# Attention and two feed-forward layers on one core: the first two blocks issued in another written order, their copies on ScalarE, products of zeros before the first scores

## The chip, the cores and the metric

The kernel runs on 1 core of one Trainium2 chip. The metric is the device time of one execution in microseconds (us), as the median over runs. A core has TensorE (PE; its weight loads are shown as PEld), VectorE (DVE), ScalarE (ACT), GpSimd (POOL) and SyncE (SP), whose queue issues all the DMAs here. Each engine works through its own queue in order and waits on semaphores.

## What is computed

Three functions in a row, on 4 x 576 = 2304 tokens, in float32 (the weights arrive as float64):

```python
x = attention(q, k, v)             # 8 heads of 64; heads 0-3: a local window of 32 keys,
                                   # heads 4-7: keys of the same residue mod 32; causal
h = x @ w_in;  x = (h - tanh(h)) @ w_out             # 512 -> 2048 -> 512
xn = x / sqrt(mean(x*x) + 1e-6) * rms_g
out = (silu(xn @ w_gate) * (xn @ w_val)) @ w_out2    # 512 -> 1536 -> 512
```

## The kernel before

The tokens are cut into nine blocks of 256, and the blocks into groups (0,1), (2,3), (4), (5,6), (7,8). For each group the attention of its blocks makes `xs`, and the first feed-forward layer then runs over 16 slices f of 128 columns of `w_in`: a unit (g, f, a, e) is `pe_h` (12 products into `ps_h`), `act_tanh`, `dve_g`, `g_hi` (ScalarE), `g_lo` (VectorE), and `pe_x` (12 products with a slice of `w_out` into `ps_x`). To keep float32 precision every operand stands as a high part (a copy in fp32r) and a low part (the rest), and a product is three: high by high, high by low, low by high.

A weight is converted while group 0 is worked on, one 128 x 512 slice at a time. `Weight.bits`: a scaling of the raw bits (`ca`, on GpSimd for the first five, on ScalarE later), then three operations on VectorE (lines 169 to 173) that put the 32 bits together (`ct`). `Weight.split`: the high part by ScalarE (line 181), the low part by VectorE (line 182). In group 0, 32 slices go this way.

Attention of a block has a local half L and a strided half D, and each half has two items 0 and 1. The stages of a half are `st_s` (scores on TensorE, preceded for the first two blocks by two products with the identity that write the mask), `st_m` (maxima, VectorE, lines 283 to 291), `st_e` (exponentials, ScalarE, line 297), `st_n` (normalisation, VectorE, lines 305 to 307), `st_p` (transposes, TensorE, line 316), `st_c` (copy out of the accumulators, line 320), `st_v` (products with v, TensorE) and `st_o` (lines 324 and 325: high part by ScalarE, low part by VectorE, into `xs`).

For the first two blocks the order is written out by hand: the string `START` is a list of words, and `first` issues them one after the other, under a manual schedule that keeps that order on each engine. `m0L1` is `st_m` of block 0, half L, item 1. Of the other words `<` lists the loads, B is the `bits` of the next weight, H its `split`, h the `pe_h` of the next unit, T its tanh and all that follows up to `g_lo`, X its `pe_x`. The last letters of p, s, v name the accumulator bank, those of c the engine. All that comes after `START` is placed by a scheduler, which also puts later work into gaps. The last two lines of the string:

```python
m1D0 e1D0 n1L0 p1L0h c1L0v T H m1D1 e1D1 n1L1 p1L1h c1L1v B h H X
n1D0 p1D0m c1D0v T n1D1 p1D1m c1D1v v1Lh o1L0 o1L1 v1Dh o1D0 o1D1 B h H T B
```

Of the kernel before, what the change touches and what calls it, by code (L numbers as in the profile page):

```python
# [32 lines left out]
def attn_moe_moe_kernel(  # L33
# [112 lines left out]
    class Weight:  # L146
# [9 lines left out]

        def bits(self, on_act):
            w = self.raw.rearrange("p c f -> p (c f)").bitcast(U32).rearrange("p (n t) -> p n t", t=2)
            lo, hi = w[:, :, 0], w[:, :, 1]
            a = cvt.tile([128, 512], F32, tag="ca", name="ca")  # L160
            if on_act:
                nc.scalar.mul(out=a, in_=hi.bitcast(F32), mul=2.0 ** -111)  # L162
            else:
                nc.gpsimd.tensor_scalar(
                    out=a, in0=hi.bitcast(F32), scalar1=2.0 ** -111, scalar2=1.0, op0=ALU.mult, op1=ALU.mult
                )
            a = a.bitcast(U32)
# [5 lines left out]
            nc.vector.scalar_tensor_tensor(  # L173
                out=t, in0=lo, scalar=29, in1=t, op0=ALU.logical_shift_right, op1=ALU.bitwise_or
            )
            self.b = t.bitcast(F32)

        def split(self, pool, tag, lo_eng):
            self.t = pool.tile([128, 2, 4, 128], F32R, tag=tag, name="w")
            t = self.t.rearrange("p s c f -> p s (c f)")  # L180
            nc.scalar.copy(out=t[:, 0], in_=self.b)  # L181
            lo_eng.tensor_tensor(out=t[:, 1], in0=self.b, in1=t[:, 0].bitcast(F32), op=ALU.subtract)  # L182

# [54 lines left out]
    class Heads:  # L238
# [586 lines left out]
    wks = [Work(groups[1])]  # L825
    xq, tq, pg = [], [], None
    banks = {"h": bank_h, "m": bank_m, "x": bank_x}
    eng = {"a": nc.scalar.copy, "v": nc.vector.tensor_copy}

    def first(word):  # L830

        op, rest = word[0], word[1:]
        if op == "<":
            for c in rest:
                loads[c]()
        elif op in "BH":
            if op == "B":
                st1.ws[st1.i].bits(False)
                st1.i += 1
            else:  # L840
                k = next(k for k, w in enumerate(st1.ws) if not hasattr(w, "t"))
                pool, tag, e = st1.place(k)
                st1.ws[k].split(pool, tag, e)
        elif op == "h":
            tq.append(units.pop(0))
            pe_h(*tq[-1])
        elif op == "T":
            u = tq.pop(0)
            for fn in (act_tanh, dve_g, g_hi, g_lo):
                fn(*u)  # L850
            xq.append(u)
        elif op == "X":
            pe_x(*xq.pop(0))
# [204 lines left out]
```

## Time and profile before

| | before |
|---|---|
| median of 3 runs | 972.84 us (972.03 to 973.92) |
| the profiled execution | 970.39 us, span of its instructions 968.6 us |
| busy, share of the span: PE, DVE, ACT, POOL | 95%, 60%, 35%, 17% |
| the chain that ended last: PE, DVE, DMA, POOL | 83%, 9%, 4%, 2% |
| instructions in the span | 13634 |

The span runs from the first to the last instruction of the profiled execution; 1.8 us of its time lie around the span. Busy TensorE counts each product with the whole time that it is in flight, and products overlap, so a stage in which TensorE is always busy need not be one in which it works at its peak. The granted clock of TensorE (PEclk) is 1.0 for 2.4 GHz and 0.5 for 1.2 GHz; there is no record of it before 22.6 us of this execution, and the views show 1.0 there.

### The profile page before, as it was taken

To read this page: it belongs to the slowest core of one execution; us is meant where nothing else is said; L and a number is where in the kernel's file an instruction comes from. 1 tells how busy PE (TensorE), PEld (TensorE's weight loads), DVE (VectorE), ACT (ScalarE), POOL (GpSimd) and SP (SyncE) were. 2 spreads that over 40 slices of the span, in tenths; PEclk is the share of its full clock that TensorE was granted. 3 is DMA by queue.
4 is the path that set the end of the run, shared out by engine and by line. 5 is a ranking of instruction groups with operands and counts; after the bars stand their busy time and mean duration, and the time that the engine had idled before them with its cause. 6 is when DMAs were issued, how large, how long until landed. Compare 5 with 4: busy or idle time off the path is not lost.

```text
span 968.6 us, 13634 instructions
## 1 busy us (share of the span) xinstructions
PE 920.4 (95%) x5242; PEld 762.5 (79%) x5242; DVE 579.8 (60%) x1270; ACT 343.0 (35%) x787; POOL 160.0 (17%) x216
## 2 busy tenths in 40 slices
PE   4589998799989999999999999999999999999998
PEld 2478776588879978888888888888888888888897
DVE  4569899998576898728999865245123512231212
ACT  3346664332245332336656423113111311121111
POOL 0000023678232767300000000000000000000000
PEclk9679999999999999999999999999999999999999
DMA  9536342331132210017536211101010000000000
GB/s 280 142 131 234 114 141 87 106 109 39 33 97 82 77 46 17 1 61 243 184 121 221 64 64 44 44 0 44 1 44 1 22 1 23 22 1 1 33 12 23
DMA packets 33731, 72.87 MB, mean 75 GB/s; under 512 B 6977, under 2 KB 15553, under 8 KB 33665
## 3 DMA queue, kind: packets, MB, share of 16 engines
q1 hardware_dynamic: 33664, 71.99, 22.9%
q8 instruction: 41, 0.67, 0.3%
q14 instruction: 26, 0.20, 0.1%
HBM read 62.54 MB, written 9.44 MB: 74 GB/s over the span
## 4 chain that ended last, share of the span: by engine, by line
PE 83%; DVE 9%; DMA 4%; POOL 2%; issue 1%; ACT 1%; SPq 0%; ACTq 0%; DVEq 0%
PE ps_x L142 32%; PE ps_h L142 32%; PE ps_m L142 16%; DVE so L523 2%; DMA raw<-in_w_in_dram 2%; POOL pr L483 2%; PE ps_v L142 1%; PE ps_p L316 1%; DVE g L674 1%; DMA raw<-in_w_out_dram 1%; PE ps_s L142 1%; DVE tg L663 1%; DVE w L182 1%; DVE sc L488 1%; DVE ct L173 1%
## 5 line engine op out<-in xcount | busy, mean ns | idle before, releaser
L142 PE MATMUL ps_x<-g,w 128*128 128x512 f32 (+1 forms) x984 | 218.3, 371 | 7.7 <-DVE w L182 4.4
L142 PE MATMUL ps_h<-xs,w 128*128 128x512 f32 (+1 forms) x984 | 222.1, 375 | 2.1 <-DVE w L182 1.1
L142 PEld LDWEIGHTS ps_x<-g,w 128*128 128x128 f32 x984 | 170.5, 191 | 40.4 <-DVE w L182 5.5
L142 PEld LDWEIGHTS ps_h<-xs,w 128*128 128x128 f32 x984 | 174.2, 196 | 34.5 <-ACT w L181 1.8
L773 DVE SCALAR_TENSOR_TENSOR s<-ps_m,s 128x512 f32<-128x512 f32 (+1 forms) x60 | 38.3, 638 | 222.4 <-PE ps_m L142 222.1
L142 PE MATMUL ps_h<-xn,w 128*128 128x512 f32 (+1 forms) x720 | 159.1, 369 | 0.0
L142 PE MATMUL ps_m<-xn,w 128*128 128x512 f32 (+1 forms) x720 | 158.4, 368 | 0.0
L142 PE MATMUL ps_x<-w,p 128*128 128x512 f32 x648 | 157.8, 391 | 0.0
L142 PEld LDWEIGHTS ps_h<-xn,w 128*128 128x128 f32 x720 | 126.8, 188 | 24.5
L142 PEld LDWEIGHTS ps_m<-xn,w 128*128 128x128 f32 x720 | 126.0, 188 | 23.1
L142 PEld LDWEIGHTS ps_x<-w,p 128*128 128x128 f32 x648 | 120.7, 188 | 25.6
L483 POOL TENSOR_TENSOR pr<-sk,sq 128x256 f32<-128x256 f32 (+1 forms) x101 | 84.2, 867 | 128.6 <-DMA sk<-in_k_str_dram 88.9
L772 ACT ACTIVATE s<-ps_h 128x512 f32<-128x512 f32 (+1 forms) x60 | 33.3, 556 | 163.6 <-PE ps_h L142 163.3
L516 POOL TENSOR_TENSOR pr<-sv,se 128x288 f32<-128x288 f32 (+12 forms) x104 | 71.2, 707 | 68.6 <-DVE so L523 20.3
L775 ACT CAST p<-s 128x512 fp32r<-128x512 f32 (+1 forms) x60 | 34.6, 577 | 122.5 <-DVE s L773 122.5
L669 ACT CAST g<-tg 128x512 fp32r<-128x512 f32 (+1 forms) x82 | 46.6, 568 | 87.2 <-DVE tg L663 86.9
L663 DVE SCALAR_TENSOR_TENSOR tg<-ps_h,tg 128x512 f32<-128x512 f32 (+1 forms) x82 | 50.7, 618 | 35.9 <-ACT tg L658 35.9
L658 ACT ACTIVATE tg<-ps_h 128x512 f32<-128x512 f32 (+1 forms) x82 | 44.5, 543 | 78.0 <-PE ps_h L142 77.7
L523 DVE TENSOR_REDUCE so<-pr 128x16 f32<-128x240 f32 (+11 forms) x104 | 64.8, 651 | 6.6 <-POOL pr L516 6.2
L674 DVE TENSOR_TENSOR g<-tg,g 128x512 fp32r<-128x512 f32 (+1 forms) x82 | 58.2, 709 | 12.3 <-ACT g L669 11.9
L776 DVE TENSOR_TENSOR p<-s,p 128x512 fp32r<-128x512 f32 (+1 forms) x60 | 38.3, 638 | 25.9 <-ACT p L775 25.6
L162 ACT ACTIVATE ca<-raw 128x512 f32<-128x512 f32 x63 | 42.4, 674 | 31.6 <-DVE ct L170 14.9
(77 smaller groups left out, 682.7 us busy)
## 6 DMA issues: line engine op xcount, KB each, us to landing
raw<-in_w_out_dram SPq DMA_DIRECT2D x28, 512.0 KB, 5.3
raw<-in_w_in_dram SPq DMA_DIRECT2D x16, 512.0 KB, 7.5
raw<-in_w_gate_dram SPq DMA_DIRECT2D x12, 512.0 KB, 3.6
raw<-in_w_val_dram SPq DMA_DIRECT2D x12, 512.0 KB, 3.5
x2d<-xe SPq DMA_DIRECT2D x36, 128.0 KB, 2.0
x<-x2d SPq DMA_DIRECT2D x16, 256.0 KB, 4.0
out_dram<-o SPq DMA_DIRECT2D x16, 256.0 KB, 2.0
sk<-in_k_str_dram SPq DMA_DIRECT2D x4, 576.0 KB, 3.8
```

What stands on the lines that cost most here:

```text
L142: nc.tensor.matmul(out_, lhsT, rhs, start=start, stop=stop, skip_group_check=True)
L162: nc.scalar.mul(out=a, in_=hi.bitcast(F32), mul=2.0 ** -111)
L483: nc.gpsimd.tensor_tensor(out=pr, in0=self.k[:, a:e, :], in1=self.q[:, c - c0:c - c0 + 1, :].to_broadcast([128, e - a, D]), op=ALU.mult,)
L516: nc.gpsimd.tensor_tensor(out=pr, in0=self.v[:, 0:c + 1, a:e], in1=self.e[:, c - c0, 0:c + 1].unsqueeze(2).to_broadcast([128, c + 1, e - a ...
L523: pend.append(lambda: nc.vector.tensor_reduce(out=o[:, c - g0, a:e], in_=pr.rearrange("l c d -> l d c"), axis=AX.X, op=ALU.add))
L658: nc.scalar.activation(out=t, in_=h_of[g, f, a], func=ACTF.Tanh, scale=WS)
L663: nc.vector.scalar_tensor_tensor(out=t, in0=h_of.pop((g, f, a)), scalar=WS, in1=t, op0=ALU.mult, op1=ALU.subtract)
L669: nc.scalar.copy(out=t[:, 0], in_=t_of[g, f, a])
L674: nc.vector.tensor_tensor(out=t[:, 1], in0=t_of.pop((g, f, a)), in1=t[:, 0].bitcast(F32), op=ALU.subtract)
L773: nc.vector.scalar_tensor_tensor(out=s, in0=r[1], scalar=WS, in1=s, op0=ALU.mult, op1=ALU.mult)
L775: nc.scalar.copy(out=t[:, 0], in_=s)
L776: nc.vector.tensor_tensor(out=t[:, 1], in0=s, in1=t[:, 0].bitcast(F32), op=ALU.subtract)
```

## The change

`START` is replaced by another list. The same words' work is in it, five scalings and five mergings of weights, four splits, three `pe_h`, three tanh and one `pe_x`, the eight copies, in another order and cut finer. B is now A (scaling, GpSimd) and B (the three VectorE operations); H is P (high part, ScalarE) and Q (low part, VectorE); T is T, G, I, J (tanh, `dve_g`, `g_hi`, `g_lo`); o is y (high part) and z (low part). Numbers after the letters name the weight or the unit. All eight copies c go to ScalarE; before, VectorE did them. The loads are in another order: the first raw weight comes after the v's of block 0 and not before them. A new word W9 clears a tile and multiplies it with itself nine times on TensorE (bf16, 128 x 512), ahead of all other products.

```diff
 START = """
-<tabwcdwAwBCDwwww2ww
-s0Lx s0Dx m0L0 e0L0 m0L1 e0L1 m0D0 e0D0 m0D1 e0D1 B
-n0L0 p0L0h c0L0v n0L1 p0L1h c0L1v H s1Lx n0D0 p0D0m c0D0v m1L0 e1L0
-v0Lh o0L0 o0L1 n0D1 p0D1m c0D1v m1L1 e1L1 v0Dh o0D0 o0D1 s1Dm h B
...
+<tabcdwABwCDwww2ww
+W9
+s0Lx m0L0 s0Dx m0L1 m0D0 e0L0 m0D1 e0L1 n0L0 p0L0h0 A0 e0D0 n0L1 B0 p0L1h1 c0L0a s1Lx c0L1a e0D1 n0D0 v0Lh0
+P0 n0D1 p0D0m0 y0L0 A1 p0D1m1 y0L1 z0L0 c0D0a z0L1 s1Dx c0D1a Q0 v0Dh1 m1L0 m1L1 y0D0 y0D1 z0D0 A2 e1L0 z0D1
+m1D0 h0h0 e1L1 n1L0 m1D1 p1L0m0 T0 G0 c1L0a n1L1 I0 e1D0 J0 p1L1m1 B1 c1L1a e1D1 n1D0 P1 n1D1 p1D0m0 Q1
+c1D0a p1D1m1 B2 v1Lm0 A3 c1D1a v1Dm1 y1L0 y1L1 z1L0 P2 h1h1 z1L1 y1D0 Q2 y1D1 z1D0 A4 X0 T1 z1D1 G1 h2h0 B3
+I1 T2 J1 P3 G2 Q3 I2 J2 B4
 """
...
+        elif op == "W":
+            z = att.tile([128, 512], F32, tag="sm", name="zero").bitcast(BF16)[:, :512]
+            nc.vector.memset(z, 0.0)
+            ps = bank_of("m0")("ps_w")
+            for _ in range(int(rest)):
+                mm(ps, z[:, :128], z, True, True)
...
+        elif op in "ABPQ":
+            w = st1.ws[int(rest)]
+            pool, tag, e = st1.place(int(rest))
+            if op == "A":
+                w.scale(nc.gpsimd)
...
             elif op == "c":
-                fn(int(rest[0]), eng[rest[1]])
+                fn(int(rest[0]), nc.scalar.copy)
```

`scale`, `merge`, `high`, `low`, `st_y` and `st_z` are the two halves of `bits`, `split` and `st_o`, with the same operations. Line numbers after line 21 are 3 to 34 higher in the changed kernel.

The order on VectorE around the first normalisations, before (names: `nm` maxima, `ct` and `ca` a weight's bits, `ss` and `sm` sums and exponentials, `ps_p` transposed, `pT` its copy):

```order
L283 TENSOR_REDUCE nm<-ps_s 128x2 x2
L291 TENSOR_SCALAR nm<-nm 128x4
L169 TENSOR_SCALAR ct<-ca 128x512
L170 SCALAR_TENSOR_TENSOR ct<-ca,ct 128x512
L173 SCALAR_TENSOR_TENSOR ct<-raw,ct 128x512
L305 TENSOR_SCALAR ss<-ss 128x4
L306 RECIPROCAL ss<-ss 128x4
L307 TENSOR_TENSOR sm<-sm,ss 128x384
L320 COPY pT<-ps_p 96x512
L305 TENSOR_SCALAR ss<-ss 128x4
L306 RECIPROCAL ss<-ss 128x4
L307 TENSOR_TENSOR sm<-sm,ss 128x384
```

and in the changed kernel:

```order
L298 TENSOR_REDUCE nm<-ps_s 128x2 x2
L306 TENSOR_SCALAR nm<-nm 128x4
L320 TENSOR_SCALAR ss<-ss 128x4
L321 RECIPROCAL ss<-ss 128x4
L322 TENSOR_TENSOR sm<-sm,ss 128x384
L320 TENSOR_SCALAR ss<-ss 128x4
L321 RECIPROCAL ss<-ss 128x4
L322 TENSOR_TENSOR sm<-sm,ss 128x384
L174 TENSOR_SCALAR ct<-ca 128x512
L175 SCALAR_TENSOR_TENSOR ct<-ca,ct 128x512
L178 SCALAR_TENSOR_TENSOR ct<-raw,ct 128x512
L320 TENSOR_SCALAR ss<-ss 128x4
```

The first weight has moved behind the two normalisations of half L, and the copy between them is gone from VectorE.

The order on TensorE from the last product with the mask of block 1's half L on, before (`lq` queries and keys, `v` and `dv` values of the halves L and D, `tab` the mask):

```order
L142 MATMUL ps_s<-tab 128x384
L142 MATMUL ps_s<-lq 64x96 x16
L316 MATMUL ps_p<-tab,sm 64x128 x4
L142 MATMUL ps_v<-pT,v 64x64 x16
L316 MATMUL ps_p<-tab,sm 64x128 x4
L142 MATMUL ps_v<-pT,dv 32x64 x32
```

and in the changed kernel:

```order
L145 MATMUL ps_s<-tab 128x384
L145 MATMUL ps_s<-lq 64x96 x16
L145 MATMUL ps_v<-pT,v 64x64 x16
L331 MATMUL ps_p<-tab,sm 64x128 x8
L145 LDWEIGHTS tab
L145 MATMUL ps_s<-tab 128x256
```

The products with `v` now come ahead of all eight transposes of half D, and where the products with `dv` stood the mask of block 1's half D begins, with the scores that follow it.

VectorE later in group 0, behind the written list, where the scheduler sets the order, before (`w` a weight's low part, `tg` and `g` of a unit):

```order
L169 TENSOR_SCALAR ct<-ca 128x512
L170 SCALAR_TENSOR_TENSOR ct<-ca,ct 128x512
L663 SCALAR_TENSOR_TENSOR tg<-ps_h,tg 128x512
L182 TENSOR_TENSOR w<-ct,w 128x512
L173 SCALAR_TENSOR_TENSOR ct<-raw,ct 128x512
L169 TENSOR_SCALAR ct<-ca 128x512
L674 TENSOR_TENSOR g<-tg,g 128x512
```

and in the changed kernel:

```order
L178 SCALAR_TENSOR_TENSOR ct<-raw,ct 128x512 x2
L696 TENSOR_TENSOR g<-tg,g 128x512
L189 TENSOR_TENSOR w<-ct,w 128x512 x2
L174 TENSOR_SCALAR ct<-ca 128x512 x2
L175 SCALAR_TENSOR_TENSOR ct<-ca,ct 128x512 x2
L685 SCALAR_TENSOR_TENSOR tg<-ps_h,tg 128x512
L178 SCALAR_TENSOR_TENSOR ct<-raw,ct 128x512
```

The weights, which took turns with a distance of half a conversion, now go through the same steps two by two.

## Rows read from the trace of the kernel before

**Rows 1.** The page's first part: busy time, share and instructions of each engine.
```profile
PE 920.4 (95%) x5242; PEld 762.5 (79%) x5242; DVE 579.8 (60%) x1270; ACT 343.0 (35%) x787; POOL 160.0 (17%) x216
```

**Rows 2.** Stages: busy us (instructions) of PE, PEld, DVE, ACT, POOL; PEclk, DMA, GB/s.
```profile
0.00:66.60 66.60, 38.54 (x448) 29.97 (x449) 36.47 (x110) 24.03 (x101) 4.57 (x11) 0.77 0.58 173
66.60:181.40 114.80, 104.96 (x702) 80.73 (x701) 107.43 (x250) 65.89 (x152) 22.43 (x24) 0.98 0.41 140
181.40:400.00 218.60, 212.57 (x1457) 181.79 (x1456) 176.73 (x469) 81.28 (x234) 133.03 (x181) 0.99 0.22 66
400.00:968.60 568.60, 564.37 (x2641) 470.07 (x2639) 259.22 (x443) 171.84 (x300) 0.00 (x0) 1.00 0.16 54
```

**Rows 3.** Chain that ended last, in time: start us, us, what.
```profile
26.62 9.31 DMA raw<-in_w_out_dram
...
192.46 2.72 PE ps_h L142 x12
```

**Rows 4.** Timeline, VectorE: start us, us, instruction, [idle <-releaser].
```profile
6.62 0.62 DVE L283 TENSOR_REDUCE nm<-ps_s 128x2 f32<-128x192 f32 x2 [5.75 <-PE ps_s L142]
...
8.34 0.36 DVE L283 TENSOR_REDUCE nm<-ps_s 128x2 f32<-128x192 f32 x1 [0.89 <-ACT sm L297]
...
12.60 0.42 DVE L169 TENSOR_SCALAR ct<-ca 128x512 uint32<-128x512 uint32 x1
...
14.39 0.62 DVE L305 TENSOR_SCALAR ss<-ss 128x4 f32<-128x4 f32 x1
...
37.13 0.16 DVE L305 TENSOR_SCALAR ss<-ss 128x4 f32<-128x4 f32 x1
...
37.53 0.56 DVE L307 TENSOR_TENSOR sm<-sm,ss 128x384 f32<-128x384 f32 x1
...
66.15 0.42 DVE L674 TENSOR_TENSOR g<-tg,g 128x256 fp32r<-128x256 f32 x1
```

**Rows 5.** VectorE groups to 66.6: xcount | busy us, mean ns | idle.
```profile
L325 DVE TENSOR_TENSOR xs<-ps_v,xs 128x256 fp32r<-128x256 f32 x8 | 4.1, 513 | 8.6 <-ACT xs L324 8.6
...
L320 DVE COPY pT<-ps_p 96x512 f32<-96x512 f32 x4 | 2.7, 686 | 4.5 <-PE ps_p L316 4.5
...
L286 DVE CUSTOM_DVE_ANT_0 sm<-ps_s,tab 128x96 f32<-128x96 f32 x8 | 1.6, 252 | 0.0
```

**Rows 6.** Timeline, TensorE.
```profile
3.68 0.82 PE L142 MATMUL ps_s<-tab 128*128 128x384 bf16 x2 [3.68 <-DMA tab<-in_tabs_dram]
...
5.01 1.56 PE L142 MATMUL ps_s<-lq 64*64 64x96 f32 x32 [0.51 <-DMA lq<-in_near_l_dram]
...
15.96 1.06 PE L316 MATMUL ps_p<-tab,sm 128*96 128x128 f32 x4 [7.42 <-DVE sm L307]
...
32.89 3.43 PE L142 MATMUL ps_h<-xs,w 128*128 128x256 f32 x12
...
43.87 2.83 PE L142 MATMUL ps_h<-xs,w 128*128 128x256 f32 x12
...
54.49 1.98 PE L142 MATMUL ps_v<-pT,v 96*64 96x64 f32 x32
...
67.94 0.60 PE L316 MATMUL ps_p<-tab,sm 128*96 128x128 f32 x4
```

**Rows 7.** Timeline, ScalarE: first and last record of one block half's exponentials.
```profile
7.55 0.34 ACT L297 ACTIVATE sm<-ps_s,nm 128x96 f32<-128x96 f32 x1 [5.32 <-DVE nm L291]
...
8.73 0.21 ACT L297 ACTIVATION_READ_ACCUMULATOR sm<-ps_s,nm 128x1 f32 x1
```

**Rows 8.** Line 320, copies: duration ns min/median/max, start us.
```profile
L320 ACT COPY pT<-ps_p x20: 571/582/598, 68.7 to 396.8; 96x512 f32<-96x512 f32 x14, 64x512 f32<-64x512 f32 x4, 128x512 f32<-128x512 f32 x2
```

**Rows 9.** Stage as in rows 2, from the first clock record to 66.6.
```profile
22.60:66.60 44.00, 29.87 (x338) 24.28 (x336) 26.78 (x82) 16.64 (x66) 2.17 (x2) 0.65 0.40 123
```

**Rows 10.** Timeline, GpSimd: second scaling of a raw weight.
```profile
14.34 0.65 POOL L164 TENSOR_SCALAR ca<-raw 128x512 f32<-128x512 f32 x1 [2.98 <-DMA raw<-in_w_in_dram]
```

**Rows 11.** VectorE groups, 66.6 to 181.4: low parts of weights.
```profile
L182 DVE TENSOR_TENSOR w<-ct,w 128x512 fp32r<-128x512 f32 x28 | 20.0, 715 | 1.5 <-ACT w L181 1.5
```

More of the change, by code (lines that the diff above doesn't have):

```diff
@@ L173, in bits, with high, low @@
             nc.vector.scalar_tensor_tensor(
-                out=t, in0=lo, scalar=29, in1=t, op0=ALU.logical_shift_right, op1=ALU.bitwise_or
+                out=t, in0=self.lo, scalar=29, in1=t, op0=ALU.logical_shift_right, op1=ALU.bitwise_or
             )
             self.b = t.bitcast(F32)
+        def high(self, pool, tag):
+            self.t = pool.tile([128, 2, 4, 128], F32R, tag=tag, name="w")
+            nc.scalar.copy(out=self.t[:, 0].rearrange("p c f -> p (c f)"), in_=self.b)
+        def low(self, eng):
+            t = self.t.rearrange("p s c f -> p s (c f)")
+            eng.tensor_tensor(out=t[:, 1], in0=self.b, in1=t[:, 0].bitcast(F32), op=ALU.subtract)
+        def bits(self, on_act):
+            self.scale(nc.scalar)
+            self.merge()
         def split(self, pool, tag, lo_eng):
[L179 to L182, printed above, removed]
+            self.high(pool, tag)
+            self.low(lo_eng)
     class Stream:
@@ L320, in st_c, with st_y, st_z @@
             copy(out=pT, in_=self.pp.pop(i))
+        def st_y(self, i):
+            nc.scalar.copy(out=self.dst(i)[0], in_=self.po[i])
+        def st_z(self, i):
+            dst = self.dst(i)
+            nc.vector.tensor_tensor(out=dst[1], in0=self.po.pop(i), in1=dst[0].bitcast(F32), op=ALU.subtract)
         def st_o(self, i):
-            dst = self.dst(i)
-            nc.scalar.copy(out=dst[0], in_=self.po[i])
-            nc.vector.tensor_tensor(out=dst[1], in0=self.po.pop(i), in1=dst[0].bitcast(F32), op=ALU.subtract)
+            self.st_y(i)
+            self.st_z(i)
     class Local(Heads):
@@ L825, in attn_moe_moe_kernel, with bank_of @@
     wks = [Work(groups[1])]
-    xq, tq, pg = [], [], None
-    banks = {"h": bank_h, "m": bank_m, "x": bank_x}
-    eng = {"a": nc.scalar.copy, "v": nc.vector.tensor_copy}
+    xq, first_units, pg = [], units[:3], None
+    del units[:3]
+    def bank_of(tag):
+        if tag == "x":
+            return bank_x
+        return lambda name: {"h": ps_h, "m": ps_m}[tag[0]].tile([128, 512], F32, tag=tag, name=name)
     def first(word):
@@ L835, in first @@
                 loads[c]()
[L836 to L839, printed above, removed]
-            else:
-                k = next(k for k, w in enumerate(st1.ws) if not hasattr(w, "t"))
-                pool, tag, e = st1.place(k)
-                st1.ws[k].split(pool, tag, e)
+        elif op == "W":
[9 more added lines that the diff above has]
+                w.scale(nc.gpsimd)
+            elif op == "B":
+                w.merge()
+                st1.i = int(rest) + 1
+            elif op == "P":
+                w.high(pool, tag)
+            else:
+                w.low(e)
         elif op == "h":
[L845 to L853, printed above, removed]
+            pe_h(*first_units[int(rest[0])], bank_of(rest[1:]))
+        elif op in "TGIJX":
+            u = first_units[int(rest)]
+            {"T": act_tanh, "G": dve_g, "I": g_hi, "J": g_lo, "X": pe_x}[op](*u)
+            if op == "J":
+                xq.append(u)
+            if op == "X":
+                xq.remove(u)
         else:
```

27 lines of the change are left out of this document (13 added, 14 removed).

## The prediction, made before the changed kernel was run

> **What bounds the kernel now.** I read the page's busy shares first: TensorE is busy 95% of the span, VectorE 60% [rows 1]. That is a mean over stages with different limits, so I cut the span into stages next [rows 2]. In the last one, 400 to 968.6 us, TensorE is busy 564.37 of 568.6 us and VectorE less than half: there the end is set by products, 12 of 512 columns in 2.72 us one after the other in the chain of waits [rows 3]. From 181.4 to 400 TensorE has 212.57 of 218.6. From 66.6 to 181.4 VectorE is the fuller engine for its kind, 107.43 of 114.8 us (94%): it converts the weights. Only in the first 66.6 us is everyone idle much of the time: VectorE works 36.47 us, ScalarE 24.03, TensorE is in flight 38.54. That stage is the written list. Nothing behind it has room for more than a few us, so what the list loses or saves should reach the end.
>
> The chain puts the time up to 35.93 us on loads of weights [rows 3]. I don't trust that label: VectorE meanwhile goes from one instruction to the next, and where it idles the timeline names TensorE and ScalarE, not a load [rows 4]. The waits inside the list are of three kinds. The second maximum waits until the first exponentials have read the scores (8.34 us) [rows 4]. The first normalisation starts at 14.39, though its exponentials ended at 8.94 [rows 7]: two maxima and a weight (12.60 to 14.39) stand ahead of it [rows 4]; TensorE idles 7.42 us for it [rows 6]. And VectorE stands 4.5 us before four of its eight copies, waiting for transposes it has nothing to do with otherwise, and 8.6 us before the low parts of the attention's result, waiting for ScalarE [rows 5].
>
> **The sum.** I lay the new list out by hand. Its lengths: a maximum 0.93 us until its exponentials can begin (6.62 to 7.55), exponentials 1.39 (7.55 to 8.94) [rows 4, 7], a normalisation 0.96 (37.13 to 38.09), a merging 1.79 (12.60 to 14.39), a unit's elementwise operation 0.42 [rows 4]; on TensorE mask products 0.82, scores 1.56, four transposes 1.06, products with v 1.98, twelve products of 256 columns 2.83 [rows 6]. For half D I take the same, which is a little long.
>
> Nine products of zeros: 2.83/12 = 0.24 us for 256 columns gives 0.47 for 512, 4.2 us in all; at the pace of 2.72 us for twelve of 512 [rows 3] it is 2.0. Their tile is cleared behind VectorE's first instruction, so I let them start at 1.2 (estimate) and end at 3.2 to 5.4. The scores wait for a load until 5.01 anyway [rows 6]. I take 5.4, so they cost about 1.2 us: mask to 6.2, scores to 7.8, where before 6.57. Two maxima, now back to back, to 9.6; two exponentials to 12.4; normalisation 13.4 and transposes 14.4 (before, the first transposes started at 15.96 and the second three us later). From here TensorE's queue carries the chain: scores of block 1 (2.38) to 16.8, products with v to 18.8, eight transposes (2.12) to 20.9, scores D to 23.3, products with v to 25.3. Two high and two low parts at 0.51 [rows 5] end at 27.3, and the second half of the first unit (1.4) at 28.7. Before, this unit ended at 32.89 + 3.43 = 36.3 [rows 6]: 7.6 us gained.
>
> Block 1 on VectorE from 27.3: two maxima, four normalisations, two elementwise operations and a merging, 1.86 + 3.84 + 0.84 + 1.79 = 8.3, to 35.6; transposes to 36.7; products with v, 3.96, to 40.7; two units and the products with `w_out`, 8.49, to 49.2; tanh to low part, 4 x 0.42, to **50.9**. Before, that low part ended at 66.57 [rows 4]: 15.7 us earlier. In its pauses the old list also did work that is not its own, eight maxima of block 2 (1.6 us) [rows 5] and two of its normalisations (2 x 0.96): 3.5 us that come after the new list. 15.7 - 3.5 = **12.2**.
>
> All this has TensorE at the slow pace: four transposes took 1.06 at 15.96 and 0.60 at 67.94 [rows 6], and from 22.6 to 66.6 the granted clock was 0.65 [rows 9], that is 30% of the time at 2.4 GHz and 70% at 1.2. TensorE's part of the laid-out chain is 29.2 us; at the fast pace (0.60/1.06) it would be 12.6 shorter, a gain of 24.8. With the 30% that the trace shows: 12.2 + 0.3 x 12.6 = **16.0**. These are the ends, 12.2 and 24.8; I take 16.0 because the old stage's clock is the nearest row.
>
> The Trainium skill (TensorE: Matmul & The Clock Gate, Part 1) says that the slow clock is the default, that activity lifts it and that an idle engine falls back. By it the zeros would make only the first mask and scores fast (1.0 us of 2.38 saved) and be undone in the wait for the first normalisation; the sum would be 17.0. No row here shows products before 3.68, and the sum stays 16.0.
>
> What costs nothing, and its cover. The eight copies take 0.58 on ScalarE [rows 8] instead of 0.69 on VectorE [rows 5]; ScalarE is busy 24.03 of 66.6 us [rows 2], and in the laid-out list the first copy is wanted 2 us after its transposes. Were ScalarE late, the products with v would be. The first raw weight is now the sixth load; the seventh had landed by 14.34 [rows 10]. Its scaling (0.65), merging and two normalisations (1.92) must end by 18.8, so it may land until 14.4; each us later holds VectorE's queue, and with it all of half D, by one. The other loads pass no consumer that is earlier than they were.
>
> Added to the profiled execution: 970.39 - 16.0 = 954.4. That execution lies 2.4 us below the median of the runs, 972.84, so the forecast for the median is **956.8**.
>
> **The rivals.** *TensorE fast through most of the list* (chance 0.09): the new order leaves it fewer pauses, and the three fast stretches before came in its denser parts. All 12.6 us saved: 972.84 - 24.8 = 948.0. Against it: TensorE still waits for two exponentials and a normalisation, 8 to 13 us. The rule of the Trainium skill named above (TensorE: Matmul & The Clock Gate, Part 1) speaks for it where the list is dense and against it in those waits.
>
> *The next stage takes half* (0.06): from 66.6 on the scheduler places everything, and TensorE, in flight 104.96 of 114.8 us [rows 2], may be as much its bound as VectorE; the 3.5 us of work that went into pauses and the first units then come at once. A gain of 8: 964.8.
>
> *No change* (0.03): the backlog of conversions ends when it did, because VectorE falls from 94% to about 83% of a stage of 115 us. For it speaks nothing but that no row shows that stage in the new order.
>
> *Slower* (0.03): behind the list the new order takes the weights two by two, and the low parts can wait for their high parts on ScalarE. One such operation of 512 columns takes 0.58 there [rows 8]. If each of the 28 weights waits for one and every second for another, 28 x 0.58 + 14 x 0.58 = 24.4 us are lost: 972.84 - 16.0 + 24.4 = 981.2. It decides from 16.0/28 = 0.57 us per weight. Against it: now all 28 together wait 1.5 us [rows 11].
>
> **The numbers.** My forecast, a gain between 10 and 22 us, has 0.79. Range: all at the slow pace gives 960.6, and the case of half 964.8, so I end at 965.5; at the other end a gain of 23 leaves out most of the fast case, 949.5. Outside are no more than 2 in 10. Two executions that differ by under 0.2% (1.9 us) can't be told apart here: faster 0.94 (forecast, fast and half), the same 0.03, slower 0.03.
>
> **What would show it.** Right: first transposes near 12 to 14 us and not 15.96; the first unit's products end near 29; the low part of the third unit near 50; VectorE idles some 20 us in the list and not 30; behind it VectorE is again over 90% busy until the last weight; the accumulators of group 0 are emptied 16 us before 181.4, and all later pieces of the chain stand earlier by as much. Wrong: the first merging waits for its load with normalisations behind it; copies on ScalarE stand behind exponentials while TensorE idles; or the list ends at 50 and the gain is gone by the end of group 0, which would be the third or fourth rival.

## The result

| | before | changed |
|---|---|---|
| median of 4 runs each | 972.60 us (972.03 to 973.92) | 945.26 us (944.99 to 946.48) |
| the profiled execution | 970.39 us | 945.39 us, span 943.7 us |
| ratio of the runs | | 0.972 (95% interval 0.970 to 0.974) |

The changed kernel is 27.3 us faster. The forecast was a gain of 16.0 and a range that ended at 949.5, so the direction was right and the time lies 4 us outside the range.

The page's first part of the changed kernel answers to [rows 1]:

```profile
PE 911.2 (97%) x5251; PEld 756.8 (80%) x5251; DVE 571.0 (61%) x1263; ACT 345.0 (37%) x795; POOL 159.9 (17%) x216
```

The stages of the changed kernel, cut at the same pieces of work as [rows 2] (end of the third unit's low part, first emptied accumulator of group 0; columns as there):

```profile
0.00:43.54 43.54, 31.23 (x459) 23.67 (x460) 27.49 (x81) 24.29 (x93) 4.71 (x11) 0.80 0.88 272
43.54:153.60 110.06, 101.88 (x700) 80.22 (x700) 106.66 (x269) 67.74 (x169) 18.63 (x21) 0.96 0.43 143
```

The list is over at 43.54 us and not at 66.57 (23.0 less). The stage behind it takes 110.06 and not 114.83 us (4.8 less). From the first emptied accumulator to the end it is 943.7 - 153.6 = 790.1 us and was 968.6 - 181.4 = 787.2 (2.9 more). Together 24.9, the difference of the two spans; of the other 2.4 of the 27.3, 2.2 are the distance of the old profiled execution from its median. The two moments of emptying, before and changed (duration ns, first and last start in us):

```profile
L693 ACT ACTIVATE xe<-ps_x x20: 379/598/615, 181.4 to 524.8; 128x512 f32<-128x512 f32 x16, 128x256 f32<-128x256 f32 x4
```

```profile
L715 ACT ACTIVATE xe<-ps_x x20: 378/597/615, 153.6 to 499.8; 128x512 f32<-128x512 f32 x16, 128x256 f32<-128x256 f32 x4
```

VectorE in the new list (timeline, columns as in [rows 4]; in this view several records can stand as one row):

```profile
6.29 0.62 DVE L298 TENSOR_REDUCE nm<-ps_s 128x2 f32<-128x192 f32 x2 [5.13 <-PE ps_s L145]
...
7.03 0.61 DVE L298 TENSOR_REDUCE nm<-ps_s 128x2 f32<-128x192 f32 x2
...
10.45 0.49 DVE L298 TENSOR_REDUCE nm<-ps_s 128x2 f32<-128x128 f32 x2 [2.60 <-PE ps_s L145]
...
11.65 0.16 DVE L320 TENSOR_SCALAR ss<-ss 128x4 f32<-128x4 f32 x1
...
14.04 0.43 DVE L174 TENSOR_SCALAR ct<-ca 128x512 uint32<-128x512 uint32 x1 [0.54 <-POOL ca L167]
...
43.12 0.42 DVE L696 TENSOR_TENSOR g<-tg,g 128x256 fp32r<-128x256 f32 x1
```

TensorE in the new list, answering to [rows 6]:

```profile
1.22 3.88 PE L145 MATMUL ps_w<-zero 128*128 128x512 bf16 x9 [1.22 <-DVE zero L864]
4.93 0.49 PE L145 MATMUL ps_s<-tab 128*128 128x384 bf16 x2
5.35 0.89 PE L145 MATMUL ps_s<-lq 64*64 64x96 f32 x32
...
9.71 0.69 PE L145 MATMUL ps_s<-dq 64*64 64x64 f32 x32 [3.13 <-DMA dq<-in_near_d_dram]
12.76 1.94 PE L331 MATMUL ps_p<-tab,sm 128*96 128x128 f32 x8 [2.36 <-ACT sm L312]
...
34.21 1.74 PE L145 MATMUL ps_v<-pT,v 96*64 96x64 f32 x32
...
39.96 1.60 PE L145 MATMUL ps_h<-xs,w 128*128 128x256 f32 x12
```

The zeros end at 5.10, about when the scores began before (5.01 in [rows 6]). The first two maxima stand together (6.29, 7.03). The queries and keys of half D come late (9.71; they landed at 9.66, before at 7.37), and VectorE waits 2.60 us for their scores with the normalisation of half L queued behind them. From 35.5 us to the end of the list the clock is 2.4 GHz, and a unit takes 1.60 instead of 2.83; the products with v at 34.21, most of them ahead of that, still took 1.74 where 1.98 stands in [rows 6].

What VectorE waited for in the whole list, all instructions of a line together (us in total, times, longest), before, up to 66.57:

```profile
DVE pT L320 <- PE ps_p L316: 9.1, 8, 1.4
DVE xs L325 <- ACT xs L324: 8.6, 8, 2.0
DVE nm L283 <- PE ps_s L142: 5.8, 1, 5.8
DVE nm L283 <- ACT sm L297: 2.9, 4, 1.5
```

and changed, up to 43.54:

```profile
DVE nm L298 <- PE ps_s L145: 7.7, 2, 5.1
DVE xs L342 <- ACT xs L338: 5.3, 4, 2.0
```

The first row of before was the largest: 9.1 us, 1.1 before each of the eight copies. [rows 5] shows only the four copies of one shape, with 4.5. It is gone with the copies, as is the wait of the maxima for exponentials. The wait for the first scores stayed (5.8 before, 5.1 of the 7.7 us now); the other 2.6 us are the scores of half D.

Behind the list VectorE's groups show where 4.8 us went although eight maxima and two normalisations more are done there. Before, 66.57 to 181.4 (first the low parts of g with 512 columns alone, then the reductions of strided attention, both shapes together):

```profile
L674 DVE TENSOR_TENSOR g<-tg,g 128x512 fp32r<-128x512 f32 x15 | 12.4, 827 | 0.3 <-ACT g L669 0.3
```

```profile
L488 DVE TENSOR_REDUCE sc<-pr 128x4 f32<-128x256 f32 (+1 forms) x16 | 6.6, 431 | 1.3 <-POOL pr L483 1.3
```

Changed, 43.54 to 153.6:

```profile
L696 DVE TENSOR_TENSOR g<-tg,g 128x512 fp32r<-128x512 f32 x15 | 10.2, 681 | 0.0
```

```profile
L509 DVE TENSOR_REDUCE sc<-pr 128x4 f32<-128x256 f32 (+1 forms) x12 | 5.2, 431 | 0.2 <-POOL pr L504 0.2
```

VectorE's idle time there fell from 7.4 us (114.83 - 107.46) to 3.4 (110.06 - 106.66). Its work fell by 0.8: four reductions of strided attention moved behind group 0, a low part of g with 512 columns takes 681 ns on average instead of 827, and the four operations of the 28 weights together take 69.3 us instead of 71.5.

### The profile page after: what moved, and what is told of

Its sections match the earlier page's. It is cut to its first block, busy times and chain, and to the rows that moved or that the text cites. A ratio compares the mean times of both kernels' runs of the same rounds, so it can differ in the third digit from the quotient of the medians.

```text
span 943.7 us, 13656 instructions
## 1 busy us (share of the span) xinstructions
PE 911.2 (97%) x5251; PEld 756.8 (80%) x5251; DVE 571.0 (61%) x1263; ACT 345.0 (37%) x795; POOL 159.9 (17%) x216
## 3 DMA queue, kind: packets, MB, share of 16 engines
q1 hardware_dynamic: 33664, 71.99, 23.5%
## 4 chain that ended last, share of the span: by engine, by line
PE 61%; DVE 2%; issue 0%; POOL 0%; DVEq 0%
PE ps_x L145 23%; PE ps_h L145 22%; PE ps_m L145 16%; DVE so L544 1%; DVE sm L301 0%; DVE g L696 0%; DVE tg L685 0%; PE ps_v L145 0%; DVE sm L322 0%; POOL pr L504 0%; DVE os L820 0%; POOL pr L537 0%; PE ps_p L331 0%; DVE pr L552 0%; DVE xs L563 0%
## 5 line engine op out<-in xcount | busy, mean ns | idle before, releaser
L145 PE MATMUL ps_x<-g,w 128*128 128x512 f32 (+1 forms) x984 | 221.0, 373 | 4.0 <-DVE w L189 2.1
L145 PE MATMUL ps_h<-xs,w 128*128 128x512 f32 (+1 forms) x984 | 214.4, 366 | 1.0 <-DVE xs L342 0.8
L145 PEld LDWEIGHTS ps_h<-xs,w 128*128 128x128 f32 x984 | 170.6, 190 | 31.2 <-DVE xs L342 0.9
L504 POOL TENSOR_TENSOR pr<-sk,sq 128x256 f32<-128x256 f32 (+2 forms) x101 | 83.1, 857 | 119.8 <-DMA sk<-in_k_str_dram 78.9
L696 DVE TENSOR_TENSOR g<-tg,g 128x512 fp32r<-128x512 f32 (+1 forms) x82 | 55.0, 670 | 10.2 <-ACT g L691 9.9
```

What stands on the lines that cost most here:

```text
L145: nc.tensor.matmul(out_, lhsT, rhs, start=start, stop=stop, skip_group_check=True)
L504: nc.gpsimd.tensor_tensor(out=pr, in0=self.k[:, a:e, :], in1=self.q[:, c - c0:c - c0 + 1, :].to_broadcast([128, e - a, D]), op=ALU.mult,)
L696: nc.vector.tensor_tensor(out=t[:, 1], in0=t_of.pop((g, f, a)), in1=t[:, 0].bitcast(F32), op=ALU.subtract)
```

## The experiments

Each run is timed beside the kernel before on the same chip, and the ratio is to that; runs 1 to 4, 5 to 8, 9 to 12, 13 to 16 and 17 with 18 were timed together. Differences between kernels of two such sets are given from the ratios, times 972.6 us. Emptied is the start of the first emptying of group 0's accumulators in the run's profile, busy and idle are VectorE's up to there, rest is from there to the end of the span, and slow is how long TensorE's clock was at 1.2 GHz from there on (records within the next 10 us). The profiles of runs 8, 10 and 11 lie 3 to 6 us above the medians of theirs (spans 969.6, 950.2 and 946.2 us).

The scheduler places what stands behind the list by its own times, so an edit of the list can change the order there too. By the traces every engine's order apart from the edit itself is that of the changed kernel in runs 1, 6 and 12, that of before in run 3, that of run 5 in run 2 and that of run 9 in runs 13 and 18; runs 11 and 16 differ from the changed kernel, and 15 from run 5, from the end of group 0 on, on VectorE and ScalarE alone. In runs 4, 5, 7 to 10, 14 and 17 it differs more, and what such a run gains or loses is that of the edit together with that of the new order behind it.

| run | edit | median us | ratio (95%) | emptied | busy | idle | rest | slow |
|---|---|---|---|---|---|---|---|---|
| | before | 972.6 | 1 | 181.4 | 143.9 | 37.5 | 787.2 | 1.6 |
| | changed | 945.3 | 0.972 (0.970 to 0.974) | 153.6 | 134.1 | 19.5 | 790.1 | 4.8 |
| 1 | changed, no zeros | 946.9 | 0.973 (0.971 to 0.975) | 156.9 | 132.7 | 24.2 | 789.6 | 4.5 |
| 2 | changed, copies on VectorE | 944.2 | 0.970 (0.969 to 0.972) | 154.8 | 138.0 | 16.9 | 787.6 | 0 |
| 3 | old, zeros | 972.4 | 0.999 (0.998 to 1.000) | 180.3 | 144.4 | 35.9 | 790.1 | 5.0 |
| 4 | old, copies on ScalarE | 964.3 | 0.991 (0.989 to 0.992) | 175.5 | 137.5 | 37.9 | 788.2 | 0.7 |
| 5 | new order alone | 944.1 | 0.971 (0.969 to 0.972) | 154.3 | 138.5 | 15.9 | 787.7 | 0 |
| 6 | changed, old loads | 948.4 | 0.975 (0.974 to 0.976) | 156.7 | 133.9 | 22.9 | 790.5 | 4.4 |
| 7 | changed, zeros in four waits | 948.9 | 0.976 (0.974 to 0.977) | 158.1 | 137.7 | 20.4 | 789.5 | 2.0 |
| 8 | old, zeros in five waits | 968.3 | 0.996 (0.994 to 0.997) | 181.8 | 141.2 | 40.6 | 787.8 | 0 |
| 9 | old, seven copies later | 959.2 | 0.985 (0.984 to 0.987) | 167.8 | 142.6 | 25.2 | 789.5 | 2.0 |
| 10 | changed, weight first | 949.1 | 0.974 (0.972 to 0.977) | 160.4 | 133.2 | 27.1 | 789.8 | 4.5 |
| 11 | changed, zeros at the end | 941.9 | 0.969 (0.966 to 0.972) | 157.3 | 133.4 | 23.9 | 788.9 | 0 |
| 12 | changed, copies split | 945.8 | 0.972 (0.970 to 0.974) | 155.8 | 135.6 | 20.2 | 788.7 | 0 |
| 13 | run 9 and weight later | 960.2 | 0.988 (0.986 to 0.989) | 168.5 | 142.4 | 26.1 | 789.8 | 4.6 |
| 14 | run 13 and low parts later | 963.8 | 0.991 (0.990 to 0.993) | 170.5 | 143.6 | 27.0 | 789.6 | 4.5 |
| 15 | order alone, zeros at the end | 945.2 | 0.972 (0.970 to 0.974) | 156.9 | 138.8 | 18.1 | 787.4 | 0 |
| 16 | changed, zeros at both places | 941.5 | 0.968 (0.966 to 0.970) | 151.4 | 132.7 | 18.8 | 788.1 | 0 |
| 17 | run 9 and maxima first | 955.9 | 0.981 (0.979 to 0.983) | 166.4 | 141.4 | 24.9 | 787.8 | 0 |
| 18 | four parts together | 958.2 | 0.985 (0.983 to 0.986) | 166.6 | 141.7 | 24.9 | 789.5 | 4.3 |

### Zeros, copies, or the order (runs 1 to 5)

Run 1 takes the zeros out of the changed kernel, run 2 puts its copies back on VectorE, run 5 does both and leaves the order with its loads:

```diff
-W9
...
-c0L0a
+c0L0v
...
-                fn(int(rest[0]), nc.scalar.copy)
+                fn(int(rest[0]), {"a": nc.scalar.copy, "v": nc.vector.tensor_copy}[rest[1]])
```

> The changed kernel without the products of zeros; its time was 945.3, the old kernel's 972.6. Theory A (the written order alone carries the gain, as the prediction has it): only the first mask and the scores of half L run at the slow pace again, 0.82 + 1.56 instead of 0.49 + 0.89, 1.0 us: 946 to 947. Theory B (the zeros lift TensorE's clock, and the higher share of 2.4 GHz in the list, 60% and not 30%, comes from them): 0.3 x 12.6 = 3.8 us or more are lost, 949 to 953. Theory C (group 0 ends when VectorE has done its work, so work taken off VectorE counts one for one): no VectorE work changes, as A.

> The changed kernel with the eight copies of the list on VectorE again. Theory A: VectorE idles 16 us in the list, the copies fit there: 945 to 947. Theory B: the same, TensorE's clock has nothing to do with them. Theory C: 8 x 0.69 = 5.5 us are added to VectorE's work up to the end of group 0 and all come through: 950 to 951.

> The written order (with its loads) alone: no products of zeros, copies on VectorE. So far: without zeros +1.6, copies on VectorE -1.1 in the new order, but -9.1 for the copies on ScalarE in the old one. Theory A (the order removes by itself the waits that the copies on ScalarE remove in the old order; the two overlap): 944.2 + 1.6 = 945 to 947. Theory C (each part brings its own share): copies in the new order are worth something once the zeros are gone, 950 or more.

Runs 3 and 4 put the zeros, or the copies on ScalarE, into the old kernel, with the same lines the other way round.

> The old kernel with the products of zeros alone. Theory A: mask and scores 1.0 us faster, then the old waits: 971.5 to 973. Theory B: the fast clock carries on past the scores: 967 to 970. Theory C: as A.

> The old kernel with the eight copies on ScalarE alone. Theory A: the old order keeps its waits; 2 us at most for the two copies between normalisations: 970 to 973. Theory B: as A. Theory C: 5.5 us of work leave VectorE, and with them up to 4.5 us in which it stood before copies: 962 to 967.

The order alone is as fast as the whole change (944.1 and 945.3, the intervals overlap); zeros are worth 1.1 us in the changed kernel (the intervals overlap), 1.0 in the old and 0.4 without the copies (the intervals overlap). So the order with its loads carries the gain by itself, as theory A has it. Run 4 went against theory A: 964.3 came, in the range of theory C, and not 970 to 973. The copies on ScalarE are worth 9.1 us in the old order and cost 1.7 in the new one (the intervals overlap). In the old order they took 6.4 us of work from VectorE up to the emptying, and its idle time stayed (37.5 and 37.9). In the new one (run 2 against the changed kernel) 3.9 us of work left VectorE, 2.6 came back as idle time, and the rest grew by 2.5. So theory C, by which each part brings its own share, holds in the old order and fails in the new one. What VectorE waited for in run 5, up to 45.49:

```profile
DVE nm L297 <- PE ps_s L144: 6.3, 2, 6.0
DVE xs L341 <- ACT xs L337: 2.8, 4, 1.5
...
DVE pT L334 <- PE ps_p L330: 0.3, 1, 0.3
```

The eight copies are on VectorE and it waits 0.3 us before them, not 9.1, since they stand behind other work. Theory B fails with the same run. Its clock was 1.2 GHz for 17.0 of the 28.9 us of the list that have a record (there is none before 16.6), as the stage from 23.5 to 40.5 (columns as in [rows 2]) and its products show; TensorE's timeline has the old lengths of [rows 6]:

```profile
23.50:40.50 17.00, 12.08 (x130) 9.92 (x131) 13.93 (x37) 7.54 (x34) 2.19 (x2) 0.50 0.83 279
```

```profile
33.43 1.97 PE L144 MATMUL ps_v<-pT,v 96*64 96x64 f32 x32
...
37.70 2.93 PE L144 MATMUL ps_h<-xs,w 128*128 128x256 f32 x12
```

Its third unit's low part ended at 45.49, 2 us behind that of the changed kernel, and its end came no later. In run 4 the wait before copies is gone too, but VectorE then stood longer before the low parts (8.6 us before; up to 63.7 in this run):

```profile
DVE xs L325 <- ACT xs L324: 12.3, 8, 3.5
```

### Which part of the order (runs 9, 10, 13, 14, 17, 18)

Run 9 moves seven copies in the old list, on VectorE as before, behind the next piece of VectorE's work; its first line:

```diff
-n0L0 p0L0h c0L0v n0L1 p0L1h c0L1v H s1Lx n0D0 p0D0m c0D0v m1L0 e1L0
+n0L0 p0L0h n0L1 c0L0v p0L1h H s1Lx n0D0 c0L1v p0D0m m1L0 c0D0v e1L0
```

> The old kernel with one thing of the new order: seven of the eight copies, still on VectorE, stand behind one more piece of VectorE's work (the next normalisation, maxima or merging), so that VectorE no longer stands directly behind the transposes that it waits for. In the old list it waited 9.1 us for them, in the new order with copies on VectorE 0.3 us. Theory F (the end follows VectorE's idle time up to the last weight of group 0): 6 to 9 us of it go, 963.5 to 966.5. Theory G (the waits only move to the next thing, low parts behind ScalarE or TensorE, as a share of them did when the copies went to ScalarE: 8.6 to 12.3 us there): 3 us or less, 969.5 to 972.

959.2: 14.0 us from seven words, more than theory F had. (The scheduler's order changed with them, from 44 us on also for the scores of block 2, so not all of it need be the words.) The wait before copies fell to 2.0 us (up to 55), and VectorE's idle time up to the emptying from 37.5 to 25.2, since what stood behind each copy also came earlier.

```profile
DVE pT L320 <- PE ps_p L316: 2.0, 2, 1.7
```

Run 10 undoes, in the changed kernel, the part for which the prediction had read TensorE's longest wait (7.42 us, [rows 6]):

```diff
-m0D1 e0L1 n0L0 p0L0h0 A0 e0D0 n0L1 B0 p0L1h1
+m0D1 e0L1 A0 B0 n0L0 p0L0h0 e0D0 n0L1 p0L1h1
```

> The changed kernel with the first weight's scaling and merging ahead of the first normalisations again, as the old list has it. Its raw weight lands at 11.5 to 13.2 us, the merging then ends near 14.1 to 15.9, and the first normalisation starts there and not at 9.9 to 11.7: about 4.2 us later. Theory F: the 4.2 us are idle time and waits of VectorE that nothing fills: 948.5 to 950. Theory G: half of it is caught up before the last weight: 946 to 948.

949.1, which is 2.4 us slower by the ratios (the intervals overlap) and 3.9 by the medians, between the two theories. VectorE waits 3.0 us for the scaling, behind the load:

```profile
DVE ct L174 <- POOL ca L167: 3.0, 1, 3.0
```

Runs 13, 14 and 17 add single parts to run 9, run 18 four at once:

```diff
-m0L0 e0L0 m0L1 e0L1 m0D0 e0D0 m0D1 e0D1 B
+m0L0 e0L0 m0L1 e0L1 m0D0 e0D0 m0D1 e0D1
...
-n0L0 p0L0h n0L1 c0L0v p0L1h H s1Lx
+n0L0 p0L0h n0L1 p0L1h B c0L0v H s1Lx
...
-v0Lh o0L0 o0L1 n0D1 p0D1m m1L1 c0D1v e1L1 v0Dh o0D0 o0D1 s1Dm h B
+n0D1 p0D1m v0Lh m1L1 o0L0 o0L1 c0D1v s1Dm e1L1 v0Dh B m1D0 o0D0 o0D1 h
...
-m0L0 e0L0 m0L1 e0L1 m0D0 e0D0 m0D1 e0D1 B
+m0L0 m0L1 e0L0 m0D0 e0L1 m0D1 e0D0 e0D1 B
```

> The old kernel with the copies moved back (959.2 so far) and, on top, the first weight's scaling and merging behind the first two normalisations instead of ahead of them. Theory F (the end follows VectorE's idle time): the merging's 1.8 us pass out of the wait for the first transposes, and the maximum of that wait shrinks by as much: 955.5 to 957.5. Theory G (the wait moves on): 958.5 to 960.

> As the run before, and on top the low parts of the attention's result stand behind the next normalisation, maxima or merging: VectorE waited 8.6 us for ScalarE before them in the old list and 4.4 with the copies moved. TensorE's order changes with it (the second transposes of half D ahead of the products with v, the scores of block 1 ahead of the products with dv). Theory F: 3 to 4 us more than the run before, so about 952 to 954. Theory G: VectorE waits for the same TensorE work elsewhere: within 1 us of the run before.

> The old kernel with the copies moved back (959.2) and, on top, the maxima of block 0 one after the other ahead of the exponentials that read the same scores, as the new list has them. VectorE waited 3.2 us for those exponentials there. Theory F (VectorE's idle time): 955.5 to 957.5. Theory G (the wait moves to the next thing that it needs): 958.5 to 960.

> The old kernel with four parts of the new list: copies moved back, first weight behind the normalisations, maxima first, and the new order of the loads. Each of the first two waits that are left then has its cover: the first normalisation has neither maxima nor a weight nor exponentials of another half ahead of it. Theory F (parts count together although none did alone): 950 to 955. Theory G (what is left is TensorE's order and block 1): 957.5 to 960.

(The last low parts of block 1 move in the same way in run 14.) The maxima bring 3 to 4 us (theory F): the last low part of block 1's attention ended 3.3 us earlier than in run 9 (47.9 and 51.2), with the order on TensorE still the same up to there. The weight behind the normalisations brings nothing in this order (the intervals overlap), and the low parts later cost 3.5 (both against theory F). Four parts together are no better than the copies alone. There the maxima no longer wait for exponentials (3.2 us in run 13), but VectorE waits 2.5 us for the scores of half D, whose queries and keys landed at 9.5 us and not at 7.5 as in run 17:

```profile
10.67 0.49 DVE L283 TENSOR_REDUCE nm<-ps_s 128x2 f32<-128x128 f32 x2 [2.48 <-PE ps_s L142]
```

So copies and maxima make 17 of the 28 us, with what the scheduler made of them; the rest is not settled by single parts. Most of it lies in the list, which ended at 56.5 us in run 18 and at 45.5 in run 5. In run 18 TensorE still stands 3.9 us before the second transposes of half D and 3.8 before those of block 1, for normalisations that the old list has behind low parts and units:

```profile
24.02 1.03 PE L316 MATMUL ps_p<-tab,sm 128*64 128x128 f32 x4 [3.94 <-DVE sm L307]
...
37.40 1.09 PE L316 MATMUL ps_p<-tab,sm 128*96 128x128 f32 x4 [3.84 <-DVE sm L307]
```

### Loads, and TensorE kept busy (runs 6 to 8, 12)

```diff
-<tabcdwABwCDwww2ww
+<tabwcdwAwBCDww2ww
```

> The changed kernel with the first raw weights back among the first loads, ahead of the v's. In the changed kernel the queries and keys of half D landed at 9.66 us (7.37 before) and VectorE idled 2.60 us for the scores of half D, with both normalisations of half L queued behind the maxima. Theory A: they land near 7.4 again, the first normalisation starts up to 1.5 us earlier, and the end with it: 943.5 to 945. Theory E (VectorE's queue then waits elsewhere, for the exponentials or for the v's that land later): 945 to 947.

2.7 us slower, more than either theory had. The queries and keys of half D landed earlier here (8.12 us), but those of block 1 later (15.60 instead of 14.49), and TensorE, with the products with v queued behind, waited for them:

```profile
15.65 1.56 PE L145 MATMUL ps_s<-lq 64*64 64x96 f32 x32 [1.39 <-DMA lq<-in_near_l_dram]
```

Run 7 adds words such as W24 ahead of four waits of TensorE in the changed kernel, run 8 does so in the old one.

```diff
-s0Lx m0L0 s0Dx
+s0Lx m0L0 W24:m1 s0Dx
```

> The changed kernel with products of zeros (256 columns) also in four of TensorE's waits: 24 before the scores of half D, 16 before the first transposes, 6 and 20 before those of block 1. Theory B (the clock is a large part of the gain: TensorE's part of the laid-out chain took 20.4 us and not 29.2, and at 2.4 GHz throughout it takes 16.6): up to 3.8 us more, 941.5 to 943. Theory A (the order; what TensorE saves there VectorE and ScalarE wait away): 944.5 to 946.

> The old kernel with products of zeros (256 columns) before the first scores and in five of TensorE's waits: 52 and 14 before the first two transposes, 34, 34 and 12 before later ones. Order, copies and loads are the old ones. Theory B (the clock by itself): the slow 70% of 12.6 us come back, 8.8: 964 to 966. Theory A: TensorE is not what the old order waits for, so a faster TensorE saves 1 to 4: 969 to 972.

In run 7 the clock was at 2.4 GHz from 6.5 to 37.2 us and the last low parts of block 1's attention ended at 35.1 and not 39.4 us. But the scheduler, which places what follows by its own times, then put scores of block 2 between the units of the list, with a pause of 1.29 us among them for which the profile shows no cause ("issue"). The third unit ended at 43.9, the accumulators were emptied 4.5 us later than in the changed kernel, and the run is 3.6 us slower, outside both expectations; what the clock alone is worth it does not tell. TensorE in run 7:

```profile
34.45 0.38 PE L145 MATMUL ps_s<-lq 64*64 64x96 f32 x4
36.12 0.71 PE L145 MATMUL ps_s<-lq 64*64 64x96 f32 x12 [1.29 <-issue]
```

Run 8 gained 4.2 us, half of what theory B had and between the two ranges; with the order behind the list changed as well, that is no clean price of the clock.

> The changed kernel with the four copies of block 0 on VectorE and the four of block 1 on ScalarE. VectorE idles between 7 and 25 us of the list, where it then waits for ScalarE (5.3 us before low parts with all copies on ScalarE, 2.8 with all on VectorE), and has no idle time from 25.1 to 35. Theory F: 2.7 us of work leave VectorE against all copies there (944.1), and no wait comes back: 941.5 to 943. Theory G: what VectorE no longer does it waits for: 943.5 to 945.5.

Run 12 (the words c0 with v, c1 with a) is no faster than the changed kernel (945.8 and 945.3), which is nearest to theory G.

### The end of group 0 (runs 11, 15, 16)

```diff
         w, t = w1["out", f].t, g_of.pop((g, f, a))
+        if g == 0 and f in (14, 15):
+            z = zero["z"]
+            for _ in range({14: 8, 15: 20}[f]):
+                mm(xacc[g][0][:, :256], z[:, :128], z, False, False)
```

> The changed kernel with products of zeros (256 columns, added to the open accumulators) ahead of the last two products with w_out of group 0: 8 and 20. There TensorE waits 1.01, 1.61 and 1.05 us for the last weights, its clock is 1.2 GHz from 151.6 to 158.4, and the accumulators are emptied at 153.6: the end comes 790.1 us behind that, in the profiles without such a fall behind the emptying 787.2 to 787.8. Theory H (the 2.5 us that the changed kernel gives back after group 0 are this fall): 942.5 to 943.5. Rival (they are the later attention work of block 3 and 4, four maxima groups of which moved behind group 0): 945 to 946.5.

> The order alone (no zeros at the start, copies on VectorE: 944.1) with the 8 and 20 products of zeros at the end of group 0 that took the changed kernel from 945.3 to 941.9. In the profile of the order alone the clock was back at 2.4 GHz when the accumulators were emptied (153.2 against 154.3), so little was lost there. Theory H (what the zeros give is the fall of the clock behind the emptying): nothing to gain, 943.5 to 944.5. Rival (the zeros help the stage itself, as much in either kernel): 940.5 to 941.5.

> The changed kernel with the zeros at the end of group 0 (941.9) and 16 more each before the scores of half D and before the first transposes, which leave the order of everything else as it is. They should hold the clock at 2.4 GHz from 11.6 to 18.5 us, where the products took 1.94 + 0.85 + 1.56 + 1.91 = 6.3 us and would take about 3.5. Theory B (TensorE is on the path there): 2 to 2.8 us, 939 to 940. Theory F (what sets the end is VectorE, and it is busy or waits for ScalarE there): 941 to 942.5.

TensorE of the changed kernel at the end of group 0, and its clock there:

```profile
146.54 2.12 PE L145 MATMUL ps_x<-g,w 128*128 128x512 f32 x8 [1.01 <-DVE w L189]
150.27 0.49 PE L145 MATMUL ps_x<-g,w 128*128 128x512 f32 x1 [1.61 <-ACT g L691]
151.82 5.56 PE L145 MATMUL ps_x<-g,w 128*128 128x512 f32 x11 [1.05 <-DVE w L189]
```

```profile
151.60:158.40 6.80, 6.45 (x14) 4.75 (x15) 4.55 (x14) 2.51 (x5) 4.20 (x5) 0.50 0.40 88
```

and of run 16:

```profile
145.79 2.14 PE L145 MATMUL ps_x<-g,w 128*128 128x512 f32 x8 [0.22 <-DVE w L189]
147.77 2.36 PE L145 MATMUL ps_x<-zero 128*128 128x256 bf16 x20
...
150.88 2.56 PE L145 MATMUL ps_x<-g,w 128*128 128x512 f32 x10 [0.30 <-DVE g L696]
```

```profile
149.40:158.40 9.00, 8.70 (x42) 6.95 (x41) 6.95 (x18) 3.57 (x7) 5.63 (x7) 1.00 0.49 153
```

Three waits of 1.0 to 1.6 us, two for the last weights and one for a unit's high part, stand around the fall of the clock at 151.6, and 11 products took 5.56 us where 10 take 2.56. With zeros in the waits it stayed up: 941.9 (run 11) and 941.5 (run 16). The interval of run 16 lies below that of the changed kernel, that of run 11 overlaps with it. Of the 4.2 us between the spans of run 16 and the changed kernel 1.1 lie in the list, 1.1 in the stage behind it and 2.0 behind the emptying. In the kernel whose clock did not fall past the emptying (run 5) the same zeros bring nothing (run 15). That is theory H, for about half of the gain of run 16. The table shows it throughout: the eight profiles with 4.3 to 5.0 us of slow clock behind the emptying have a rest of 789.5 to 790.5, the nine with 0.7 or less 787.4 to 788.9, and the three between 787.2 to 789.5. The rival, attention work that moved behind group 0, does not explain it: run 12 has the changed kernel's order but for the engine of four copies, its clock did not fall past the emptying, and its rest is 788.7; runs 1 and 6 have that order and the fall, and 789.6 and 790.5.

Run 16 is the fastest kernel of the study, 0.4% below the changed one. That it is no faster than run 11 fits theory F, but its other zeros were to take away a slow stretch from 11.6 to 18.5 us and only moved it, to 14.1 to 20.9. What the clock in the list is worth with the same order behind it stays open; in run 7 it was 4.3 us at the end of block 1's attention.

## Why the prediction was wrong in size and right in direction

**Right.** The place, the first 66.6 us, and the kind of cause, VectorE standing in its queue before things that came too early in it. The maxima back to back (run 17) and the earlier transposes (12.76 instead of 15.96) are as read. The weight ahead of the normalisations cost 2.4 us in the new order (run 10, the intervals overlap) and nothing in the old one (run 13). The idle time in the list was to fall from 30 to 20 us; it fell to 16. For the zeros the prediction named 1.0 us, saved on mask and first scores; run 3 measured 1.0, and the rows show it, 0.49 + 0.89 instead of 0.82 + 1.56. The Trainium skill (TensorE: Matmul & The Clock Gate, Part 1) says that activity lifts the slow clock; this trace agrees. That the zeros would cost 1.2 us was wrong: the scores ended at 6.24 and not at 7.8.

**Wrong, the sum, by terms.** Predicted was 15.7 for the list and 0.3 x 12.6 = 3.8 for the clock: 19.5. Measured is 23.0, 3.5 more. Predicted was 3.5 lost behind the list; measured is 4.8 gained, 8.3 more. Predicted was that all behind group 0 only shifts; it gave 2.9 back. 16.0 + 3.5 + 8.3 - 2.9 = 24.9. And the 2.4 us between the old profiled execution and its median were added to the forecast, though the changed kernel has no such distance.

**The step that failed most** is "3.5 us that come after the new list. 15.7 - 3.5 = 12.2": work that moves out of pauses was priced as added to a stage of fixed length. That stage ends when VectorE has made the last weight's low part. It got 4.8 us shorter: VectorE's idle time there fell by 4.0 us and its work by 0.8, although the maxima and normalisations that came on top took 5.1 us by VectorE's groups and not 3.5. Which part of the edit cut the idle time there is not shown. VectorE's work and idle time up to the emptying is the sum to price: 143.9 + 37.5 us before, 138.5 + 15.9 with the order alone. Such a sum holds for any engine; it tells something for VectorE because the emptying starts 1.3 to 1.9 us behind the last weight's low part in 16 of the 20 profiles (181.4 and 180.1 before, 153.6 and 151.8 changed; up to 4.1 in the other four).

**The second** is "12.2 + 0.3 x 12.6": the clock was taken as the scale of the gain, 12.2 to 24.8. The order alone gained 28.4, beyond both ends, with the clock at 2.4 GHz on record in two stretches of 6.9 and 5.0 us of its 45.5 (run 5), 26% where the sum has 30%. Run 7, with the clock up to 37.2 us, was no faster, though the order behind its list differs. The laid-out list was too long for another reason: the normalisation was placed behind two exponentials (12.4), but each item needs its own only, and in run 5 it began at 9.89 us.

**"The eight copies ... cost nothing"** was right for the changed kernel and hid the largest single cause. The row that it took, 4.5 us before "four of its eight copies", is one shape of two. All eight waited 9.1 us, and moving seven of them behind other work is worth 14.0 (run 9, with what the scheduler made of it).

**"The other loads pass no consumer that is earlier than they were"** was wrong for half D: its queries and keys landed at 7.2 to 9.8 us in eleven profiles with the new loads (the changed kernel, runs 1, 2, 5, 7, 10 to 12, 15, 16, 18) and at 6.5 to 8.1 in nine with the old ones. Yet the new order needs its loads: with the old ones it is 2.7 us slower (run 6).

## What to carry to other kernels

Where an engine is the bound of a stage further on, count its idle time in everything before it, over all shapes of a line, and look for instructions that stand directly behind the other engine's work that they wait for: one piece of other work between them was worth more here (14.0 us, run 9) than the move to another engine (9.1 us, run 4). What changes are worth doesn't add: the same move gained nothing in the new order, so price each alone and both together. Where the bounding engine changes, look at TensorE's clock at the seam, and fill its last waits with products that add zero.

## What was not expected of the hardware

The clock at a seam, above: three waits of 1.0 to 1.6 us in front of a stage bound by TensorE cost that stage 1 to 2 us.

Equal lists of loads landed at different times: the queries and keys of half D between 7.2 and 9.8 us in the profiles with the new list. A difference of 2 us in the first 15 us of two profiles says little about their orders.

A low part of g (128 x 512) took 1.22 us instead of 0.68 when it began while GpSimd was in a product; between 66.57 and 181.4 of before, four of them did (1.21 to 1.24). One case, in the timeline of before:

```profile
141.71 1.76 POOL L483 TENSOR_TENSOR pr<-sk,sq 128x320 f32<-128x320 f32 x2
```

```profile
142.80 1.22 DVE L674 TENSOR_TENSOR g<-tg,g 128x512 fp32r<-128x512 f32 x1
```

The Trainium skill (Trainium Architecture — The Big Picture, What this means for kernel authors) says that VectorE and GpSimd contend for a shared port, by an exclusive lock. This trace agrees as far as it goes, and in the same stage of the changed kernel two low parts that began ahead of GpSimd's product and overlapped with it took 0.67 and 0.68.
